# A planned attention + MLP kernel: the operations of pairs 0 to 17 in another order, four norms finished on VectorE, half of the value transfers shortened

## The chip, the cores and the metric

The kernel runs on one core of a Trainium2 chip. The metric is the device time of one execution in microseconds (us). Engines are named as the profile names them: PE (TensorE), ACT (ScalarE), DVE (VectorE), POOL (GpSimd), SP (SyncE, which issues most of the transfers).

## The reference

The first part is cosine attention over 8 batches, 12 heads, 448 positions and 64 dimensions; its output, 3584 rows of 768, goes through an MLP of width 2048 with a hard-swish between.

```python
q_n = q / (np.linalg.norm(q, axis=-1, keepdims=True) + 1e-06)
k_n = k / (np.linalg.norm(k, axis=-1, keepdims=True) + 1e-06)
scores = np.matmul(q_n, k_n.transpose(0, 1, 3, 2)) / tau        # tau = 0.1
attn = np.exp(scores - scores.max(-1)); attn /= attn.sum(-1) + 1e-09
x = (attn @ v).transpose(0, 2, 1, 3).reshape(3584, 768)
h = x @ w_in                                                    # 768 -> 2048
out = (h * np.clip(h + 3.0, 0.0, 6.0) / 6.0) @ w_out            # 2048 -> 768
```

## The kernel before, in words

Two heads form a pair, so there are 48 pairs, six to a batch. Two consecutive pairs share two items of load: an item is a 128 x 2 x 7 x 64 fp32 tile with q (or k) of four heads, 448 KB. Up to item 13 the even item holds q and the odd one k; from item 14 on it is the other way round.

An item goes through these steps, each with a name that the plan uses:

- LQ loads the item (SP). There are seven buffers.
- SQ squares it, on ACT, POOL or DVE (letter a, p or v). Items 0 and 1 are squared in parts.
- RE sums the squares over 64 dimensions (DVE).
- NO makes 1/(norm + eps) for both items of a pair of items, from the sums: on ACT as Ln, Exp(0.5 x), Ln(x + eps), Exp(-x), four small instructions. With the letter v, the last two are an addition and a reciprocal on DVE.
- NM multiplies the item by it and casts it to bf16 (POOL or DVE).
- TR transposes it on PE into a PSUM bank (items 0 to 13), and CQ, CK and CS copy q and k of a pair from there into SBUF. From item 14 on, XD transposes by a DMA on SP.

A pair then has four scores matmul groups SC (groups 0 to 2 with two matmuls of 64 rows, group 3 with the last 64 keys of both heads), four exponentials EX (ACT), four value groups VA (PE, summed in the one PSUM tile PV), FI (DVE: reciprocal of the sums and the product), and BK/CX, XB or XP, which bring the result transposed into xT, the MLP's input. The values of two pairs are loaded by LV in four transfers (SP; three buffers) and cast per pair by VC (POOL, ACT or DVE).

The MLP comes in units U: the first kind is six matmuls of 448 columns for 128 of the 2048 features of a batch, then UA (ACT: relu) and UV (DVE: product); the second kind multiplies by w_out. W issues one of eight weight transfers, 768 KB each as bf16, on POOL's queue. The first four bring w_in: eight units of a batch need the first two, the others need all four. WS and GL prepare sums of w_out and of the hidden activations, with which pairs of output tiles are later computed by seven products instead of eight (L740).

DP.n and D.n are n dummy matmuls on zeros (L922, 248 columns, and L917, 512 columns). Nothing reads their results.

The order of everything up to pair 17 is written out by hand in PLAN, one token for each operation (SQ.5.a.0.7: item 5 on ACT, chunks 0 to 6). Every engine, and SP's queue of transfers, takes its operations in the plan's order, and starts one when the data, buffers and banks that it needs are there. `needs` asserts that the plan's order is a possible one. OPEN ends the first part, in which scores use two double banks SC; behind it scores, transposes and units take six PSUM banks in turn (`next_bank`). From pair 18 on (FIRST) a loop emits a fixed pattern with the units of a table. The plan contains 36 units: 16 of batch 0, 14 of batch 1, six of the second kind.

Of the kernel before, what the change touches and what calls it, by code (L numbers as in the profile page):

```python
# [18 lines left out]
ORDER = "111111111111111111111111111111222222"  # L19

PLAN = [
# [36 lines left out]
]  # L58


# [1 line left out]
def kernel(  # L62
# [76 lines left out]
    def raw_buffer(j):  # L139
# [1 line left out]

    sqs = [item(NR + i) for i in range(2)]
    nrms = [const.tile([128, 7, 2, D], BF16, name=f"nrm{i}", tag=f"nrm{i}") for i in range(3)]
    n2s = [const.tile([128, 2, 14], FP32, name=f"n2{i}", tag=f"n2{i}") for i in range(2)]
    rs = [
        [const.tile([128, 2, 14], FP32, name=f"{x}{i}", tag=f"{x}{i}") for x in ("ln", "nr", "le", "r")]
        for i in range(2)
    ]
    bias = const.tile([128, 2], FP32, name="bias", tag="bias")
    eps_bias, half_bias = bias[:, 0:1], bias[:, 1:2]  # L150
# [50 lines left out]
    def load_v(d):  # L201
        needs(("VC", 2 * (d - NV)), ("VC", 2 * (d - NV) + 1))
        b, n = 2 * d // HP, 2 * d % HP
        for g in range(2):
            f = v[b, HP * g + n : HP * g + n + 2].rearrange("i (p c) d -> p i (c d)", c=7)
            t = vr[d % NV][:, 2 * g : 2 * g + 2, :, :].rearrange("p i c d -> p i (c d)")
            for half in range(2):
                o = t[64 * half : 64 * half + 64, :, (1 - half) * D : (5 - half) * D]
                nc.sync.dma_start(out=o, in_=f[:, :, 3 * half * D : (3 * half + 4) * D])

    def square(j, e, c0, n):

# [15 lines left out]
    def reduce(j, *heads):  # L228
        d = j // 2
        needs(("NO", d - 2, 1))  # L230
        sq, have = sq_of[j]
        heads = heads or (0, 1)
        if j < 2:
            assert all(7 * g + c in have for g in heads for c in range(7))
        else:
            assert sorted(have) == list(range(7))
        c = slice(7 * heads[0], 7 * heads[-1] + 7)
        nc.vector.tensor_reduce(  # L238
            out=n2s[d % 2][:, j % 2, c],
            in_=sq[:, :, :, :].rearrange("p g c d -> p (g c) d")[:, c, :],  # L240
            axis=AX.X,
            op=ALU.add,
        )
        whole("RE", j, heads)

    def norms(d, *items):
        on_vector, items = "v" in items, tuple(x for x in items if x != "v")

        needs(("NM", 2 * d - 4), ("NM", 2 * d - 3))
        items = items or (0, 1)  # L250
        for x in items:
            needs(("RE", 2 * d + x))
        it = slice(items[0], items[-1] + 1)
        ln, nr, le, r = (t[:, it, :] for t in rs[d % 2])
        nc.scalar.activation(out=ln, in_=n2s[d % 2][:, it, :], func=AF.Ln)
        nc.scalar.activation(out=nr, in_=ln, func=AF.Exp, scale=0.5)
        if on_vector:
            nc.vector.tensor_scalar(out=le, in0=nr, scalar1=EPS, scalar2=None, op0=ALU.add)
            nc.vector.reciprocal(out=r, in_=le)
        else:  # L260
            nc.scalar.activation(out=le, in_=nr, func=AF.Ln, bias=eps_bias)
            nc.scalar.activation(out=r, in_=le, func=AF.Exp, scale=-1.0)  # L262
        for x in items:
            issued.add(("NO", d, x))

    def normalise(j, e, *heads):
        d = j // 2
# [6 lines left out]
        engines[e].tensor_tensor(  # L274
            out=nrm[:, :, g, :].rearrange("p c g d -> p g c d"),
            in0=raw_of[j][:, g, :, :],
            in1=rs[d % 2][3][:, j % 2, :]
            .rearrange("p (g c) -> p g c", g=2)[:, g, :]
            .to_broadcast([128, n, 7, D]),
            op=ALU.mult,  # L280
# [31 lines left out]
        return 4 if j % 2 else 2  # L312

    def transposes(j, bank=None):
        nrm = nrm_of.pop(j)
        z, key = bank_of(bank, readers(j))
        z = z[:, :].bitcast(BF16)
# [622 lines left out]
    def whole_units(n, engines="av"):  # L940
# [4 lines left out]
                    finish_units(e)  # L945

    OPS = {
        "LQ": load_qk, "LV": load_v, "W": next_weights, "SQ": square, "RE": reduce, "NO": norms,
        "NM": normalise, "VC": vcast, "TR": transposes, "XD": crossbar, "XB": back_crossbar, "XP": back_two, "CQ": copy_q, "CK": copy_k, "CS": copy_k3, "SC": scores,
        "EX": exps, "VA": values, "FI": finish_values, "BK": back, "CX": copy_x, "U": unit, "UA": lambda: finish_units("a"), "UV": lambda: finish_units("v"),  # L950
        "GL": g_left, "WS": lambda x, *h: weight_sums(str(x), *((h[0] * KC // 2, KC // 2) if h else (0, KC))), "UU": whole_units, "D": busy, "DP": busy_pv, "OPEN": open_ring,
# [146 lines left out]
```

## Time and profile before

| | |
|---|---|
| median of 3 runs | 405.82 us (405.77 to 408.14) |
| profiled execution: span from the first to the last instruction | 403.1 us (the page gives no total beside it) |
| PE busy, of the span | 395.5 us, 98% |
| DVE, ACT, POOL busy | 286.4, 278.3, 234.0 us |
| TensorE clock granted | 1.00 |
| DMA | 65.32 MB, 91566 packets |
| value transfers | 96 of 128 KB, 4.4 us to landing (median) |
| w_in transfers | 4 of 768 KB, 10.2 us to landing (median) |

Busy times are those of one execution. A line such as `L226 POOL TENSOR_TENSOR` names the line of the kernel, the engine and the instruction; in a timeline the first column is the start in us from the beginning of the span, the second is the time from there to the end of the last one of `xN` merged instructions, and what stands in brackets is the engine's idle time before it and what ended it.

### The profile page before, as it was taken

Reading aid. Unit: us, or ns where it says so; the run is one execution under the profiler, and the core shown is the slowest. Engines: PE = TensorE matmul, PEld = TensorE weight load, DVE = VectorE, ACT = ScalarE, POOL = GpSimd, SP = SyncE. Lnnn points to the kernel's source line nnn. Section 1 sums busy time; section 2 is a strip of 40 time slices with the busy share of each in tenths; the row PEclk is TensorE's granted clock in tenths of the full one; section 3 lists DMA queues with packets and bytes.
Section 4 is the critical chain, followed back from the end, with each engine's and each line's share of the span. In section 5 each row is a group of like instructions: output and inputs, shape, how many; then the busy total and the mean of one; then the engine's idle time right before and its main releaser. Section 6 shows DMA issues by size and latency. Waiting matters only on the chain.

```text
span 403.1 us, 9619 instructions
## 1 busy us (share of the span) xinstructions
PE 395.5 (98%) x3696; PEld 234.3 (58%) x3696; DVE 286.4 (71%) x503; ACT 278.3 (69%) x609; POOL 234.0 (58%) x228
## 2 busy tenths in 40 slices
PE   7999999999999999999999999999999999999996
PEld 4666656555655556556555556555565556555563
DVE  5898768766998777776867888687656566644663
ACT  5999998798467686786858768668658755225230
POOL 7799655662384997488386865766665500510070
PEclk9999999999999999999999999999999999999999
DMA  8999989979988659786989659976963523130134
GB/s 289 281 254 257 216 247 230 156 125 230 187 213 220 139 128 228 171 222 130 180 216 212 152 130 164 182 192 145 192 154 76 112 46 67 41 79 21 26 73 99
DMA packets 91566, 65.32 MB, mean 162 GB/s; under 512 B 56064, under 2 KB 89984, under 8 KB 91520
## 3 DMA queue, kind: packets, MB, share of 16 engines
q1 hardware_dynamic: 87408, 58.02, 62.8%
q0 software_dynamic: 3712, 6.29, 9.0%
q8 instruction: 29, 0.48, 0.5%
q10 hardware_dynamic: 400, 0.39, 0.3%
q14 instruction: 17, 0.14, 0.1%
HBM read 47.19 MB, written 11.01 MB: 144 GB/s over the span
## 4 chain that ended last, share of the span: by engine, by line
PE 94%; DVE 3%; DMA 1%; ACT 0%; issue 0%; DVEq 0%; ACTq 0%
PE M L567 24%; PE M L740 17%; PE PV L462 13%; PE Y L567 6%; PE M L422 6%; PE Z L567 5%; PE Y L740 4%; PE Z L740 4%; PE M L614 3%; PE M L820 2%; PE Z L422 2%; PE PV L922 2%; PE Z L820 1%; PE Y L422 1%; DVE n L238 1%; PE SC L422 1%
## 5 line engine op out<-in xcount | busy, mean ns | idle before, releaser
L440 ACT ACTIVATE at<-M 128x448 bf16<-128x448 f32 x200 | 99.9, 568 | 16.4 <-PE M L422 14.4
L567 PE MATMUL M<-xT,w_in_sb 128*128 128x448 bf16 x522 | 110.8, 352 | 0.0
L567 PEld LDWEIGHTS <-w_in_sb 128*128 128x128 bf16 x768 | 72.0, 98 | 62.6 <-issue 2.8
L274 POOL TENSOR_TENSOR nrm<-big,r 128x896 bf16<-128x896 f32 (+1 forms) x48 | 79.5, 1662 | 26.1 <-ACT r L262 19.3
L576 ACT ACTIVATE u<-M,bias 128x448 bf16<-128x448 f32 x87 | 57.0, 655 | 25.2 <-PE M L567 24.8
L582 DVE SCALAR_TENSOR_TENSOR gT<-u,M 128x448 bf16<-128x448 bf16 x76 | 46.7, 618 | 36.8 <-ACT u L576 36.3
L226 POOL TENSOR_TENSOR big<-big 128x896 f32<-128x896 f32 (+3 forms) x39 | 63.9, 1641 | 10.9 <-DMA big<-in_k_dram 5.7
L462 PEld LDWEIGHTS <-at 128*128 128x128 bf16 (+1 forms) x1536 | 54.9, 97 | 22.8 <-issue 13.5
L462 PE MATMUL PV<-vx,at 128*128 128x65 bf16 (+1 forms) x1536 | 64.3, 194 | 0.2 <-DVE on L483 0.2
L238 DVE TENSOR_REDUCE n<-big 128x14 f32<-128x896 f32 (+1 forms) x50 | 51.7, 1041 | 5.6 <-ACT big L224 4.6
L379 POOL COPY km<-tT 64x128 bf16<-64x128 bf16 x34 | 12.8, 376 | 58.1 <-DMA tT<-nrm 45.1
L769 POOL TENSOR_TENSOR big<-big 128x384 f32<-128x384 f32 x11 | 11.8, 1076 | 54.6 <-ACT big L788 54.5
L740 PEld LDWEIGHTS <-gT 128*128 128x128 bf16 x288 | 27.8, 98 | 20.0 <-DVE gT L718 0.6
L740 PE MATMUL M<-w_out_sb,gT 128*128 128x384 bf16 x208 | 37.9, 326 | 0.1
L440 ACT ACTIVATE at<-Z 128x448 bf16<-128x448 f32 x49 | 27.7, 565 | 9.9 <-PE M L422 7.3
L483 DVE TENSOR_TENSOR on<-PV,rc 128x512 bf16<-128x512 f32 x48 | 33.2, 691 | 1.7
L293 POOL CAST vx<-big 128x512 bf16<-128x512 f32 x44 | 33.2, 757 | 1.2 <-DMA big<-in_v_dram 1.1
L422 PE MATMUL M<-tT,kz 64*128 64x448 bf16 (+1 forms) x175 | 31.6, 351 | 0.0
L740 PEld LDWEIGHTS <-gs 128*128 128x128 bf16 x224 | 21.5, 98 | 14.8 <-DVE gs L718 0.4
L567 PE MATMUL Y<-xT,w_in_sb 128*128 128x448 bf16 x132 | 28.6, 352 | 0.0
L440 ACT ACTIVATE at<-Y 128x448 bf16<-128x448 f32 x45 | 25.7, 570 | 3.1 <-PE Z L422 1.7
L740 PE MATMUL M<-w_sum,gs 128*128 128x384 bf16 x144 | 26.3, 326 | 0.0
(130 smaller groups left out, 561.7 us busy)
## 6 DMA issues: line engine op xcount, KB each, us to landing
big<-in_v_dram SPq DMA_DIRECT2D x96, 128.0 KB, 4.4
big<-in_k_dram SPq DMA_DIRECT2D x24, 448.0 KB, 4.9
big<-in_q_dram SPq DMA_DIRECT2D x24, 448.0 KB, 4.4
out_dram<-o SPq DMA_DIRECT2D x107, 96.0 KB, 2.2
w_in_sb<-in_moe_w_in_dram POOLq DMA_DIRECT2D x4, 768.0 KB, 10.2
w_out_sb<-in_moe_w_out_dram POOLq DMA_DIRECT2D x4, 768.0 KB, 9.2
tT<-nrm SPq DMA_TRANSPOSE x34, 3.3
xT<-on SPq DMA_TRANSPOSE x25, 3.8
```

Source lines behind the costliest of these rows:

```text
L226: engines[e].tensor_tensor(out=o, in0=i, in1=i, op=ALU.mult)
L238: nc.vector.tensor_reduce(out=n2s[d % 2][:, j % 2, c], in_=sq[:, :, :, :].rearrange("p g c d -> p (g c) d")[:, c, :], axis=AX.X, op=ALU.add,)
L274: engines[e].tensor_tensor(out=nrm[:, :, g, :].rearrange("p c g d -> p g c d"), in0=raw_of[j][:, g, :, :], in1=rs[d % 2][3][:, j % 2, :] . ...
L293: (engines[e].copy if e == "a" else engines[e].tensor_copy)(out=o, in_=f)
L422: nc.tensor.matmul(o, ks, qt[rows], start=True, stop=True)
L440: nc.scalar.activation(out=o, in_=x, func=AF.Exp, scale=inv_tau)
L462: nc.tensor.matmul(pv_out(j, h), at[rows, n, q_cols(i // HP, j)], vt[rows, 3 + h if name == "M" else 5 * h + int(name[1]), :], start=(name ...
L483: nc.vector.tensor_tensor(out=on[:, :, :, :].rearrange("p j h d -> p h j d"), in0=pv4[:, :, :, 0:D], in1=rc[:, :, :].to_broadcast([128, 2, ...
L567: nc.tensor.matmul(ps[:, 0:S], w_in_sb[:, cc, fc * 128 : (fc + 1) * 128], x[:, cc, 0:S], start=(cc == 0), stop=(cc == CC - 1),)
L576: nc.scalar.activation(out=u[:, :], in_=ps[:, 0:S], func=AF.Relu, bias=half_bias, scale=1.0 / 6.0)
L582: nc.vector.scalar_tensor_tensor(out=g[:, fc, c0 : c0 + S], in0=u[:, :], scalar=1.0, in1=ps[:, 0:S], op0=ALU.min, op1=ALU.mult,)
L740: nc.tensor.matmul(m, lhs[:, c, :], rhs[:, c, c0 : c0 + width], start=(base is None and c == 0), stop=(c == KC - 1), skip_group_check=True,)
```

## The change

1. The tokens of PLAN stand in another order. The first lines, up to OPEN, were

```diff
-    "LQ.1 DP.5 SQ.1.a.11.3 SQ.1.p.4.3 DP.1 SQ.1.a.0.4 LQ.0 SQ.0.p.8.6 DP.2 DP.4 LQ.3 LQ.2 SQ.1.v.7.4 RE.1.1",
-    "SQ.0.a.0.6 RE.1.0 NO.0.1 LQ.5 LQ.4 SQ.0.v.6.2 DP.6 NM.1.p.0 D.10 RE.0.1 DP.3 NM.1.p.1 RE.0.0 DP.8 NO.0.0",
-    "SQ.3.a.0.7 LV.0 DP.2 SQ.2.a.0.7 NM.0.p.0 RE.3 RE.2 NM.0.p.1 TR.1.Y DP.2 TR.0.Z CK.0.v DP.4 SQ.4.p.0.7 CQ.0.v",
-    "SQ.5.a.0.7 LQ.6 NO.1 LV.1 LQ.7 SC.0.0.0 SC.0.1.1 DP.5 DP.3 CQ.1.v EX.0.0 RE.5 RE.4 NM.3.p SC.0.2.0 CK.1.v DP.3",
-    "EX.0.1 DP.3 EX.0.2 NM.2.v DP.3 SC.0.3.1 TR.3.Y LQ.8 NO.2 EX.0.3 DP.3 SC.1.0.0 TR.2.Z EX.1.0 VC.0.v SC.1.1.1 DP.2",
-    "EX.1.1 VA.0.0 CK.2.v VC.1.v VC.3.v NM.4.p NM.5.p VA.0.1 LQ.9 SC.1.2.0 SQ.6.a.0.7 LQ.11 DP.5 DP.2 SC.1.3.1 EX.1.2",
-    "CQ.2.v LQ.10 LV.2 VA.0.2 VA.0.3 DP.3 SC.2.0.0 DP.2 EX.1.3 CK.3.v SC.2.1.1 EX.2.0 TR.4.Y SC.2.2.0 SQ.7.p.0.7",
-    "EX.2.1 RE.6 FI.0 RE.7 LV.3 VA.1.0 SQ.8.p.0.7 SC.2.3.1 CQ.3.v VC.2.v CQ.5.v VA.1.1 EX.2.2 SC.3.0.0 EX.2.3 VA.1.2",
-    "NO.3 RE.8 SC.3.1.1 CQ.4.v EX.3.0 DP.2 DP.4 EX.3.1 VA.1.3 TR.5.Z SC.3.2.0 W SQ.9.p.0.7 EX.3.2 FI.1 CK.4.v BK.0.Y",
-    "VA.2.0 SC.3.3.1 RE.9 LV.4 EX.3.3 NO.4 VA.2.1 VA.2.2 VA.2.3 SC.4.0.0 EX.4.0 NM.6.p DP.2 SC.4.1.1 SQ.10.p.0.7 W",
-    "SQ.11.p.0.7 EX.4.1 CX.0.v TR.6.Y CK.5.v FI.2 CQ.7.v VA.3.0 BK.2.Z RE.10 SC.4.2.0 EX.4.2 NM.7.p CQ.6.v VA.3.1",
-    "SC.4.3.1 DP.2 EX.4.3 CX.2.v SC.5.0.0 RE.11 VA.3.2 EX.5.0 SC.5.1.1 VA.3.3 VC.4.p SC.5.2.0 FI.3 VC.5.p EX.5.1",
-    "BK.1.Y TR.7.Z SC.5.3.1 CX.1.v CK.6.v CK.7.v VA.4.0 EX.5.2 DP.2 CS.7.v EX.5.3 BK.3.Y VA.4.1 LQ.12 CS.6.v OPEN",
+    "LQ.1 SQ.1.a.11.3 LQ.0 LQ.3 LQ.2 SQ.1.p.4.3 SQ.1.a.0.4 DP.8 LQ.5 SQ.1.v.7.4 SQ.0.a.0.6 RE.1.1 DP.2 DP.4 RE.1.0",
+    "DP.6 LQ.4 DP.5 SQ.0.p.8.6 SQ.0.v.6.2 DP.2 NO.0.1 SQ.3.a.0.7 D.10 RE.0.1 DP.3 RE.0.0 NM.1.p.0 DP.1 NO.0.0.v",
+    "NM.1.p.1 NM.0.p.1 DP.4 DP.5 SQ.2.a.0.7 DP.2 TR.1.Y RE.3 DP.3 NM.0.p.0 DP.3 LV.0 RE.2 LV.1 SQ.5.a.0.7 CK.0.v",
+    "TR.0.Z SQ.4.p.0.7 LQ.6 CQ.0.v RE.5 DP.1 CQ.1.v DP.2 SC.0.0.0 NO.1 DP.4 RE.4 EX.0.0 SC.0.1.1 SC.0.2.0 CK.1.v",
+    "NM.2.v EX.0.1 NM.3.p SC.0.3.1 LQ.7 VC.3.a DP.3 NO.2.v EX.0.2 DP.5 NM.4.p VC.1.v VC.0.v LQ.10 EX.0.3 TR.3.Y DP.1",
+    "SC.1.0.0 EX.1.0 SC.1.1.1 TR.2.Z VA.0.0 LQ.8 SC.1.2.0 SQ.6.v.0.7 EX.1.1 CK.2.a VA.0.1 SC.1.3.1 NM.5.p EX.1.2 LQ.9",
+    "VA.0.2 DP.3 CQ.2.v LQ.11 LV.2 EX.1.3 CQ.3.v SC.2.0.0 EX.2.0 VA.0.3 CK.3.v SC.2.1.1 TR.4.Y SQ.7.p.0.7 SC.2.2.0",
+    "RE.6 FI.0 RE.7 DP.1 VA.1.0 DP.3 SQ.8.p.0.7 EX.2.1 CQ.4.v CQ.5.v SC.2.3.1 TR.5.Z RE.8 EX.2.2 NO.3 VA.1.1 DP.1",
+    "EX.2.3 SC.3.0.0 EX.3.0 VA.1.2 DP.1 W VC.2.v VA.1.3 FI.1 SC.3.1.1 SC.3.2.0 BK.0.Y EX.3.1 SQ.9.p.0.7 SQ.10.p.0.7",
+    "DP.1 CK.4.v EX.3.2 SC.3.3.1 VA.2.0 RE.9 LV.3 EX.3.3 DP.4 VA.2.1 VA.2.2 SC.4.0.0 VA.2.3 NO.4 CK.5.v NM.6.p RE.10",
+    "DP.1 EX.4.0 SC.4.1.1 EX.4.1 SC.4.2.0 CX.0.v FI.2 TR.6.Y VA.3.0 SQ.11.p.0.7 BK.2.Z NM.7.p EX.4.2 SC.4.3.1",
+    "SC.5.0.0 VA.3.1 VA.3.2 W EX.4.3 EX.5.0 CX.2.v VC.4.p SC.5.1.1 RE.11 CQ.7.v LQ.12 EX.5.1 VA.3.3 SC.5.2.0 EX.5.2",
+    "TR.7.Z CQ.6.v FI.3 SC.5.3.1 BK.1.Y DP.3 VC.5.p CS.7.v EX.5.3 CX.1.v CS.6.v CK.6.v VA.4.0 VA.4.1 BK.3.Y OPEN NO.5",
     ...
```

The rest of the plan is reordered in the same way. The first unit stands behind SC.8.2 in both.

2. Some operations have another engine. To DVE's side: the norms NO.0.0, NO.2, NO.9 and NO.10 end there; SQ.6 (from ACT), NM.13, NM.14 and VC.13 (from POOL), CQ.11 and CK.12 (from ACT). To ACT: VC.3, CK.2, CK.15, CK.16 and CQ.10 (from DVE), VC.12, VC.15 and SQ.21 (from POOL). To POOL: a seventh of SQ.16 (from ACT). There are 82 narrow dummy matmuls instead of 86.

3. The value transfers leave out the 64-dimension blocks that no cast reads:

```diff
             for half in range(2):
-                o = t[64 * half : 64 * half + 64, :, (1 - half) * D : (5 - half) * D]
-                nc.sync.dma_start(out=o, in_=f[:, :, 3 * half * D : (3 * half + 4) * D])
+                n_c = 4 if g == half else 3
+                c0 = (7 - n_c) * half
+                x = 1 if g != half or half == 0 else 0
+                o = t[64 * half : 64 * half + 64, :, x * D : (x + n_c) * D]
+                nc.sync.dma_start(out=o, in_=f[:, :, c0 * D : (c0 + n_c) * D])
```

4. The five small tiles of a norm hold both of the alternating sets in one tile each, and the four instructions stand in a function of their own. `norms_two` is there but the plan has no token for it.

```diff
-    n2s = [const.tile([128, 2, 14], FP32, name=f"n2{i}", tag=f"n2{i}") for i in range(2)]
-    rs = [
-        [const.tile([128, 2, 14], FP32, name=f"{x}{i}", tag=f"{x}{i}") for x in ("ln", "nr", "le", "r")]
-        for i in range(2)
+    n2_and_r = [
+        const.tile([128, 2, 2, 16], FP32, name=x, tag=x)[:, :, :, 0:14] for x in ("n2", "ln", "nr", "le", "r")
     ]
...
+        inverse([t[:, d % 2, it, :] for t in n2_and_r], on_vector)
...
+    def inverse(tiles, on_vector):
+        n2, ln, nr, le, r = tiles
+        nc.scalar.activation(out=ln, in_=n2, func=AF.Ln)
         nc.scalar.activation(out=nr, in_=ln, func=AF.Exp, scale=0.5)
         if on_vector:
             nc.vector.tensor_scalar(out=le, in0=nr, scalar1=EPS, scalar2=None, op0=ALU.add)
             nc.vector.reciprocal(out=r, in_=le)
         else:
             nc.scalar.activation(out=le, in_=nr, func=AF.Ln, bias=eps_bias)
             nc.scalar.activation(out=r, in_=le, func=AF.Exp, scale=-1.0)
```

More of the change, by code (lines that the diff above doesn't have):

```diff
@@ L238, in reduce @@
         nc.vector.tensor_reduce(
-            out=n2s[d % 2][:, j % 2, c],
+            out=n2_and_r[0][:, d % 2, j % 2, c],
             in_=sq[:, :, :, :].rearrange("p g c d -> p (g c) d")[:, c, :],
@@ L253, in norms, with norms_two @@
         it = slice(items[0], items[-1] + 1)
-        ln, nr, le, r = (t[:, it, :] for t in rs[d % 2])
-        nc.scalar.activation(out=ln, in_=n2s[d % 2][:, it, :], func=AF.Ln)
+        inverse([t[:, d % 2, it, :] for t in n2_and_r], on_vector)
+        for x in items:
+            issued.add(("NO", d, x))
+    def norms_two(d, on_vector=None):
+        needs(*(("NM", 2 * d + x) for x in range(-4, 0)), *(("RE", 2 * d + x) for x in range(4)))
+        inverse([t.rearrange("p e i c -> p (e i) c") for t in n2_and_r], on_vector)
+        issued.update(("NO", x, y) for x in (d, d + 1) for y in range(2))
+    def inverse(tiles, on_vector):
+        n2, ln, nr, le, r = tiles
+        nc.scalar.activation(out=ln, in_=n2, func=AF.Ln)
         nc.scalar.activation(out=nr, in_=ln, func=AF.Exp, scale=0.5)
@@ L262, in norms @@
             nc.scalar.activation(out=r, in_=le, func=AF.Exp, scale=-1.0)
-        for x in items:
-            issued.add(("NO", d, x))
     def normalise(j, e, *heads):
@@ L276, in normalise @@
             in0=raw_of[j][:, g, :, :],
-            in1=rs[d % 2][3][:, j % 2, :]
+            in1=n2_and_r[4][:, d % 2, j % 2, :]
             .rearrange("p (g c) -> p g c", g=2)[:, g, :]
@@ L314, in transposes @@
     def transposes(j, bank=None):
+        needs(("NM", j))
         nrm = nrm_of.pop(j)
@@ L947 @@
     OPS = {
-        "LQ": load_qk, "LV": load_v, "W": next_weights, "SQ": square, "RE": reduce, "NO": norms,
+        "LQ": load_qk, "LV": load_v, "W": next_weights, "SQ": square, "RE": reduce, "NO": norms, "NN": norms_two,
         "NM": normalise, "VC": vcast, "TR": transposes, "XD": crossbar, "XB": back_crossbar, "XP": back_two, "CQ": copy_q, "CK": copy_k, "CS": copy_k3, "SC": scores,
```

46 rows, old and new, of the table PLAN are left out of this document.

## The prediction

> **What bounds the kernel now.** I read the page's head first, then the busy time in three stages, the timelines of PE and POOL in the first 45 us, and the time that the weight transfers took to land.
>
> ```profile
> span 403.1 us, 9619 instructions
> PE 395.5 (98%) x3696; PEld 234.3 (58%) x3696; DVE 286.4 (71%) x503; ACT 278.3 (69%) x609; POOL 234.0 (58%) x228
> ```
>
> TensorE is the bound, but "98% busy" hides the one place where something can be won. The stages below run from the first exponential (12.87) to the first MLP unit (42.85), from there to the first score of pair 18 (115.49), and from there almost to the end.
>
> ```profile
> 12.87:42.85 29.98, 29.54 (x420) 19.46 (x418) 25.73 (x60) 28.76 (x58) 28.64 (x23) 1.00 1.08 262
> 42.85:115.49 72.64, 72.64 (x714) 42.43 (x713) 55.09 (x95) 58.41 (x130) 37.85 (x35) 1.00 0.98 198
> 115.49:390.00 274.51, 274.35 (x2442) 160.09 (x2440) 193.74 (x311) 182.23 (x402) 156.10 (x147) 1.00 0.63 139
> ```
>
> The columns are length, then busy us of PE, PEld, DVE, ACT, POOL, the clock, the DMA share, GB/s. From 42.85 on PE has no hole worth a name: units of six matmuls follow at 1.14 us, which is streaming speed, so that stage cannot get shorter. In the first stage ACT (28.76 of 29.98), POOL (28.64) and DMA (share 1.08) are full, and part of PE's 29.54 is filler: 49 dummy matmuls of 0.106 us, 5.2 us in all. So the change can gain only ahead of 42.85, and only if ACT, POOL and the transfers get through their head sooner.
>
> ```profile
> 2.48 3.90 PE L922 MATMUL PV<-xT 128*128 128x248 bf16 x18 [2.48 <-DVE vx L975]
> 6.17 2.78 PE L917 MATMUL Y<-xT 128*128 128x512 bf16 x10
> 8.79 1.54 PE L922 MATMUL PV<-xT 128*128 128x248 bf16 x13
> 10.17 0.55 PE L319 MATMUL Y<-ident,nrm 128*128 128x128 bf16 x7
> ...
> 12.47 0.55 PE L422 MATMUL SC<-tT,kz 64*128 64x448 bf16 x4 [0.65 <-DVE tT L341]
> ...
> 42.85 2.43 PE L567 MATMUL M<-xT,w_in_sb 128*128 128x448 bf16 x12
> ```
>
> Fillers run back to back from 2.48: 0.207 us each at first, 0.106 us (13 from 8.79 to 10.17) once the clock has opened, at about 7.0. The first MLP unit at 42.85 is where the full stretch begins.
>
> ```profile
> 23.07 0.85 POOL L910 DMA_DIRECT2D w_in_sb<-in_moe_w_in_dram  x1
> ...
> 28.86 0.70 POOL L910 DMA_DIRECT2D w_in_sb<-in_moe_w_in_dram  x1
> 29.57 1.69 POOL L226 TENSOR_TENSOR big<-big 128x896 f32<-128x896 f32 x1
> 31.21 1.69 POOL L274 TENSOR_TENSOR nrm<-big,r 128x896 bf16<-128x896 f32 x1
> 32.84 1.16 POOL L293 CAST vx<-big 128x512 bf16<-128x512 f32 x2
> ```
>
> POOL is a closed row of 1.64 us pieces, and the two weight transfers that the first unit needs are issued in it. For the second of them:
>
> ```profile
> L910 POOL DMA_DIRECT2D w_in_sb<-in_moe_w_in_dram x1: 699/699/699, 28.9 to 28.9; - x1
> ...
> DMA to landing us min/median/max: 13.7/13.7/13.7
> ```
>
> 28.86 + 13.7 = 42.56: it landed 0.3 us ahead of the first unit. That cover is all there is.
>
> **The change, part by part.** I walk the new order through the engines with the durations of the rows.
>
> *Fillers ahead of the first score.* Before the first transposes there are now 27 + 10 wide + 15 fillers (18 + 10 + 13 before), then 6 and 3 (2 and 4). PE takes them in order: 22 cold ones to 7.0, five warm to 7.56, ten wide at 0.216 to 9.72, fifteen to 11.31, transposes of item 1 (7 x 0.056) to 11.70, six fillers to 12.34, transposes of item 0 to 12.73. The copy of q starts 0.22 us after the last and takes 0.38, so the first score starts at about 13.43 instead of 12.47: **+0.96**. In the meantime ACT gets its squares and norms done earlier (square of item 3 moves into the 0.74 us that ACT waited for DVE), so it is free at 12.15 and waits for the late score. Of the +0.96 about 0.7 is won back in pairs 0 and 1, because the four-step norm of items 4 and 5 is now two steps on ACT (saves 0.26 + 0.27) and the square of item 6 (0.84) leaves ACT, while a value cast and a key copy come to it (about 0.5 each; ACT's copies take 0.48 to 0.53).
>
> *Norms finished on DVE.* Two small operations of about 0.21 us (reciprocal row, 128x8). For items 4 and 5 they stand behind the 1.2 us normalisation of item 2 in DVE's queue: r is ready at 17.6 instead of 16.4, and POOL, which waits for it, starts item 4 at 17.65 instead of 16.52: **+1.1 on POOL**, whose row is closed after that.
>
> *Square of item 6 on DVE.* Alone it takes 1.08 us (the same operation at 108.68). It has two inputs in SBUF, and such an operation waits for a running POOL operation:
>
> ```profile
> 213.38 0.68 DVE L718 TENSOR_TENSOR gs<-gT 128x1024 bf16<-128x1024 bf16 x1
> ...
> 221.21 1.99 DVE L718 TENSOR_TENSOR gs<-gT 128x1024 bf16<-128x1024 bf16 x1
> ```
>
> 0.68 with POOL idle, 1.99 with POOL working (a square at 220.96, then a normalisation that took 2.14 instead of 1.69). Here POOL is full, so bounds are 0 and 1.3 us for DVE, and 0 and 1.1 us for POOL (one DVE operation). I take 0.5 and 1.1. POOL's square of item 7 then begins at 22.05 instead of 19.81.
>
> *Weight transfers.* The first is issued behind the square of item 8, at 25.3 (23.07 before). The second stood behind the square of item 10; now it also stands behind the square of item 11 and the normalisation of item 7, 2 x 1.64 us: issue at 34.4 instead of 28.86. By the three of four that did not start behind another, landing takes 9.8 to 10.4 us; the second of before landed 9.7 after the first. So it lands at 44.2 to 44.8, I take 44.5, and the first unit starts at 44.6: **+1.75**. The bounds are 7.3 us (the last weight transfer, on an emptier DMA: 41.7, no wait) and 13.7 (48.1, +5.3). The Trainium skill, "DMA: Bandwidth & Descriptors", section on the anatomy of one DMA on the gpsimd path, fits 2.0 us plus bytes at 436 GB/s; for 1.57 MB read that is, as an estimate, 5.6 us and no wait. The rows of this case, 7.3 to 14.4 us, do not agree, and they decide; by the Trainium skill's figure the wait would drop out.
>
> *The other chain to the first unit* (scores of pair 8, whose exponential frees the bank): POOL's lateness reaches the reduction of item 7, so the norms of items 6 and 7 start about 1.1 later and the first exponential of pair 3 is at 26.3 (24.96). ACT is paced from there, so the exponentials of pair 6 start at 37.2 (36.12), and the first unit could start at 43.9. It is hidden behind the weights by 0.7; if they come early, +1.05 is left.
>
> *Value transfers.* 48 of 96 move 96 instead of 128 KB: 1.57 MB of 65.32. Their number, and so SP's issues, stays at 96. Six pairs of heads load ahead of 42.85: 0.39 MB, 1.5 us of a full DMA at 262 GB/s. Only about 0.1 MB falls into the second weight transfer's window, against two q/k loads that now come earlier there. Bounds -0.4 to +0.4 on its landing; I take 0.
>
> *The full stretch.* The instruction order holds the same real matmuls from the first unit to pair 18. Changes between 64-row scores and 128-row work cost 0.1 us each (the last transpose at 17.02 streams 0.06 us, the score behind it starts at 17.17); by the order there are 47 instead of 45 of them: **+0.2**. Two normalisations move from POOL to DVE (1.08 to 2.7 each; DVE has 17 us free there), four casts and copies and a square to ACT (some 2 us net, 14 free). Summed along the order, ACT from the second exponential of pair 8 to the first of pair 11 has 16.8 us against PE's 16.1, but 1.75 us of waiting for the weights lets it catch up. Bounds 0 and 4.3; I take **0.3**.
>
> *Sum:* 1.75 + 0.2 + 0.3 = +2.25 on the span of 403.1, 405.35. The page has no total for this execution; the median 405.82 lies 2.72 above its span. So 405.82 + 2.25 = **408.1**.
>
> **The rivals.**
> 1. *The weights come in time.* As the last two did (7.3 and 7.6 us), they land at 42.0 or sooner; the score chain sets the first unit at 43.9. +1.05 + 0.5: 407.4. For it: fewer value bytes. Against: DMA share 1.08 at that time. The Trainium skill's fit, named above, would give this case too.
> 2. *Faster: ACT's gaps close.* In the first stage ACT was idle 1.22 us of 29.98, and its list gets 0.37 shorter. If it never waits after its start at 13.85 (+0.96), the first unit comes 1.22 + 0.37 - 0.96 = 0.6 us sooner, at 42.2, and with the +0.2 the time is 405.4. It decides if the second weight transfer is issued by 34.4 and lands in under 7.7 us and POOL loses nothing to DVE's square. Against: r for item 4 waits behind a DVE normalisation.
> 3. *The full stretch loses its cover.* ACT's local excess over PE (0.7 up to pair 11, 0.6 in pair 12, 0.8 in pair 15: 2.1 us) and two 1.1 us waits of DVE's moved normalisations land on the bank releases that PE needs: +4.3 - 0.3 on top of the sum, 412.1. For it: ACT at 58.4 of 72.6, uneven. Against: before ran the part up to pair 11 with ACT's sum at 0.96 of PE's, and PE had no such wait.
>
> **How the numbers follow.** Forecast 0.40 (own range 406.6 to 409.9), rival 1 0.20, rival 2 0.11, rival 3 0.29. A measurement of this kernel tells about 1%, 4.1 us, from no change, so forecast and rival 1 count as the same: same 0.65, slower 0.33 (rival 3 and the forecast's upper end), faster 0.02 (PE's full stretch leaves no room for it). Range 405.2 to 412.0: from rival 2 to rival 3, leaving out the upper half of the latter and weights that land as late as 13.7 us.
>
> **What would show it.** The first 64-row score at 13.4, not 12.5; POOL's normalisation of item 4 near 17.6; DVE's square of item 6 over 1.08 us; the second weight issue near 34, its landing near 44.5 and PE's first unit right behind it with a wait on DMA; pair 18's first score near 117.7; from there the same 287 us to the end. A first unit ahead of 42.85, or waits of over 1 us on ACT or DVE behind it, would prove me wrong.

## The result, and the profile after

The changed kernel takes 410.42 us (median of 7 executions, 408.22 to 411.18) against 405.82 of the kernel before on the same chip (7 executions, 404.95 to 408.14): a ratio of 1.0097, 95% interval 1.0069 to 1.0124. The interval leaves out 1, so the loss is real, though it is just under the 1% that the prediction called the same. The forecast of 408.1 is 2.3 us short; 410.42 lies in the range, but outside the forecast's own part of it. The profiled execution took 408.59 and its span is 406.6, against 403.1 before. In the changed kernel the lines of the functions have numbers 11 higher, so the scores are L433 and the MLP's first product is L578.

The head of the page and the three stages, with columns as before (from the first exponential to the first unit, to the first score of pair 18, to almost the end):

```profile
span 406.6 us, 9623 instructions
PE 394.7 (97%) x3692; PEld 234.7 (58%) x3692; DVE 291.1 (72%) x514; ACT 277.9 (68%) x603; POOL 227.8 (56%) x223
```

```profile
13.12:43.62 30.50, 27.76 (x402) 18.26 (x401) 26.54 (x62) 28.50 (x56) 28.30 (x22) 1.00 1.00 260
43.62:119.15 75.53, 73.11 (x715) 42.71 (x714) 58.62 (x104) 58.61 (x127) 32.13 (x33) 1.00 0.93 183
119.15:393.66 274.51, 274.33 (x2443) 160.17 (x2441) 193.17 (x310) 182.48 (x403) 155.17 (x144) 1.00 0.60 135
```

The third window was cut to the length that it had before. What can be compared is the time from pair 18's first score to the end of the span: 287.5 us, against 287.6 before. The first unit comes 0.77 us later (43.62, 42.85 before). The second stage, which "cannot get shorter", got 2.89 us longer (75.53, 72.64 before), and PE is idle in it for 2.4 us where it had no idle time. These 2.4 us, in two pieces, are called the hole below. 0.77 + 2.89 = 3.66 is the delay of pair 18.

The timelines of PE and POOL ahead of the first unit (start, time to the end of the last, in brackets the idle time before):

```profile
2.47 4.60 PE L933 MATMUL PV<-xT 128*128 128x248 bf16 x27 [2.47 <-DVE vx L986]
6.91 2.32 PE L928 MATMUL Y<-xT 128*128 128x512 bf16 x10
9.06 1.75 PE L933 MATMUL PV<-xT 128*128 128x248 bf16 x15
...
12.71 0.36 PE L433 MATMUL SC<-tT,kz 64*128 64x448 bf16 x2 [0.16 <-DVE tT L352]
...
43.62 1.31 PE L578 MATMUL M<-xT,w_in_sb 128*128 128x448 bf16 x6
```

```profile
16.77 4.18 POOL L284 TENSOR_TENSOR nrm<-big,r 128x896 bf16<-128x896 f32 x2 [2.18 <-DVE r L271]
20.92 3.31 POOL L227 TENSOR_TENSOR big<-big 128x896 f32<-128x896 f32 x2
24.18 0.85 POOL L921 DMA_DIRECT2D w_in_sb<-in_moe_w_in_dram  x1
...
33.26 0.70 POOL L921 DMA_DIRECT2D w_in_sb<-in_moe_w_in_dram  x1
```

The two normalisations at 16.77 take 4.18 instead of 3.34: DVE's square of item 6 holds them up. The second weight transfer is issued at 33.26 and lands after

```profile
DMA to landing us min/median/max: 8.4/8.4/8.4
```

at 41.66, two microseconds ahead of the first unit. In the second stage PE's waits, DVE's longest wait (us in total, times, longest), the last two weight transfers, and SP's queue around the two transposes of items 14 and 15 read

```profile
PE Y L433 <- DMA tT<-nrm: 1.4, 1, 1.4
PE PV L473 <- DVE on L494: 0.9, 1, 0.9
```

```profile
DVE kz L380 <- DMA tT<-nrm: 3.5, 1, 3.5
```

```profile
72.72 0.81 POOL L921 DMA_DIRECT2D w_out_sb<-in_moe_w_out_dram  x1
...
75.18 0.81 POOL L921 DMA_DIRECT2D w_out_sb<-in_moe_w_out_dram  x1
```

```profile
76.23 1.34 SPq L341 DMA_TRANSPOSE tT<-nrm  x1
77.67 0.52 SPq L195 DMA_DIRECT2D big<-in_q_dram  x1
78.33 4.20 SPq L341 DMA_TRANSPOSE tT<-nrm  x1
```

and before

```profile
70.41 2.63 SPq L330 DMA_TRANSPOSE tT<-nrm  x2
```

The first transpose landed 8.6 us after its issue, at 84.8, the second 10.1 us after, at 88.4; before, they were issued at 70.41 and 71.8 and landed 6.3 and 5.7 us later. DVE's copy of k of pair 14 waited for the first, so FI of pair 12 behind it was late for the values of pair 13 (0.9); then the scores of pair 14 waited for the second (1.4). Two things now stand ahead of the second transpose: the weights, and the load of item 21 (448 KB, issued at 77.67, landed at 87.5), which the kernel before issues behind both transposes.

### The profile page after: what moved, and what is told of

Same layout as the page of the kernel before. It is cut to its first block, busy times and chain, and to the rows that moved or that the text cites. A ratio compares the mean times of both kernels' runs of the same rounds, so it can differ in the third digit from the quotient of the medians.

```text
span 406.6 us, 9623 instructions
## 1 busy us (share of the span) xinstructions
PE 394.7 (97%) x3692; PEld 234.7 (58%) x3692; DVE 291.1 (72%) x514; ACT 277.9 (68%) x603; POOL 227.8 (56%) x223
## 4 chain that ended last, share of the span: by engine, by line
PE 86%; DMA 4%; DVE 3%; ACT 3%; POOL 2%; issue 1%; SPq 0%; POOLq 0%; ACTq 0%
PE M L578 23%; PE M L751 16%; PE PV L473 11%; PE Y L578 6%; PE M L433 5%; PE Z L578 5%; PE Y L751 4%; PE Z L751 3%; PE M L625 3%; DMA tT<-nrm 2%; PE M L831 2%; PE Z L433 2%; POOL nrm L284 1%; PE Z L831 1%; PE Y L433 1%; DMA big<-in_q_dram 1%
## 5 line engine op out<-in xcount | busy, mean ns | idle before, releaser
L578 PE MATMUL M<-xT,w_in_sb 128*128 128x448 bf16 x516 | 109.4, 352 | 0.2 <-DMA xT<-on 0.2
L451 ACT ACTIVATE at<-M 128x448 bf16<-128x448 f32 x196 | 97.4, 565 | 16.7 <-PE M L433 14.6
L578 PEld LDWEIGHTS <-w_in_sb 128*128 128x128 bf16 x768 | 72.0, 98 | 62.5 <-issue 2.5
L284 POOL TENSOR_TENSOR nrm<-big,r 128x896 bf16<-128x896 f32 (+1 forms) x46 | 76.3, 1662 | 24.3 <-DVE r L271 12.7
L227 POOL TENSOR_TENSOR big<-big 128x896 f32<-128x896 f32 (+4 forms) x39 | 62.9, 1615 | 10.8 <-DMA big<-in_k_dram 7.6
L451 ACT ACTIVATE at<-Z 128x448 bf16<-128x448 f32 x52 | 29.5, 568 | 9.3 <-PE M L433 9.0
L303 POOL CAST vx<-big 128x512 bf16<-128x512 f32 x41 | 29.4, 723 | 8.6 <-DMA big<-in_v_dram 7.5
L433 PE MATMUL M<-tT,kz 64*128 64x448 bf16 x172 | 31.1, 351 | 0.6 <-DVE kz L352 0.5
L578 PE MATMUL Y<-xT,w_in_sb 128*128 128x448 bf16 x132 | 28.6, 352 | 0.0
```

The source lines that it names most:

```text
L227: engines[e].tensor_tensor(out=o, in0=i, in1=i, op=ALU.mult)
L284: engines[e].tensor_tensor(out=nrm[:, :, g, :].rearrange("p c g d -> p g c d"), in0=raw_of[j][:, g, :, :], in1=n2_and_r[4][:, d % 2, j % 2, :]
L303: (engines[e].copy if e == "a" else engines[e].tensor_copy)(out=o, in_=f)
L433: nc.tensor.matmul(o, ks, qt[rows], start=True, stop=True)
L451: nc.scalar.activation(out=o, in_=x, func=AF.Exp, scale=inv_tau)
L578: nc.tensor.matmul(ps[:, 0:S], w_in_sb[:, cc, fc * 128 : (fc + 1) * 128], x[:, cc, 0:S], start=(cc == 0), stop=(cc == CC - 1),)
```

## The experiments

Two questions: what makes the hole at 85 to 88 us, and what sets the first unit. All ratios are to the kernel before in the same set of runs. A loss in the full stretch is pair 18's first score minus the first unit, less the 72.64 us of before.

**e1: the last two weight transfers late.** The changed kernel, with the last two W moved back.

```diff
-SQ.16.p.0.6 UA EX.13.0 W UV U RE.16 U
+SQ.16.p.0.6 UA EX.13.0 UV U RE.16 U
-EX.13.2 UA W VC.14.p UA NO.8 SC.13.3 CS.14.v NM.16.p EX.13.3
+EX.13.2 UA VC.14.p UA NO.8 SC.13.3 CS.14.v W NM.16.p W EX.13.3
```

> The changed kernel, with the last two w_out transfers issued behind the transposes of items 14 and 15 (before the k copy of pair 14 and behind the normalisation of item 16) instead of ahead of them. Theory A (the hole of 2.7 us on PE at 85.5 to 88.5 comes from the transfers that fill the DMA engines while the two transposes wait): the second transpose lands within 7 us instead of 10.1, the hole is gone, and the time falls by 2.5 us from 410.4 to about 407.9, 1.005 of before. Theory B (the transposes are late because DVE finishes item 14 only at 76.2, 2.04 us with a wait for POOL, and the weights have nothing to do with it): the hole stays, 410.4.

408.24, ratio 1.0066 (1.0049 to 1.0084). The transposes, issued at 76.0 and 78.0 as late as before the edit, now landed in 2.6 to 4.5 us and the hole is gone. But 2.28 us of the full stretch stay lost: PE waits for DVE, 0.9 us up to 97.6 and 0.5 up to 101.7. So the transfers' place explains the hole, and moving them alone gives most of it back later. In the profile's chain of what released what, the first of these waits goes back to

```profile
88.98 7.35 DMA tT<-nrm
```

This is the next transpose. It landed at 96.33, just behind the last weight transfer, which was issued at 87.17 and landed at 95.36; in the changed kernel, with no weights ahead of it, it took 2.7 us. DVE's copy out of it stands ahead of the product that PE waits for. So the same collision came back one pair of items later.

**e2: item 14 normalised on POOL.** The changed kernel with `NM.14.p` for `NM.14.v`.

> The changed kernel, with one letter changed: item 14 is normalised on POOL again. The transpose of item 14 is then issued near 71.5 instead of 76.2, and POOL issues the last two w_out transfers 1.6 us later. Theory A (DMA engines full of weights): the first transpose lands before the weights flow, the second partly; the hole shrinks to 0 to 1 us, 408 to 409. Theory B (late normalisation): the hole is gone, 407.8. If moving it costs POOL something elsewhere, 410 or more.

406.78, ratio 1.0034 (1.0021 to 1.0047). The transposes were issued at 71.8 and 73.8 and landed by 80.8; the loss of the full stretch is 0.30, less than either theory gave. The last two weight transfers now went out behind the transposes, at 74.8 and 77.2. One letter gives back 0.63% of the 0.97%.

**e3: the kernel before with the last two W early**, right behind its NM.15.p.

> The kernel before, with the last two w_out transfers issued directly behind the normalisation of item 15 (near 67) instead of at 78.0 and 85.7; nothing else. Theory A: the transposes of items 14 and 15, issued at 70.4 and 71.7, no longer land in 5.7 to 6.8 us but only when the weights are through, near 85 to 88; PE gets a hole of 1 to 4 us ahead of the scores of pair 14, and the time is 407 to 410. Theory B: no change, 405.8.

405.71, ratio 1.0009 (0.9986 to 1.0031). The transposes landed 11.8 and 12.4 us after their issue at 71.9 and 73.3, at 84.3 and 85.1, slower than in any other run: as in theory A, they landed only when the weights were through (84.2). The full stretch lost 1.10 in the profile, with 0.9 us of waiting on PE, but the median does not show it.

**e4: the kernel before with the shortened value transfers alone** (part 3 of the change).

> The kernel before with the shortened value transfers alone (48 of 96 move 96 instead of 128 KB). The forecast took this part at nothing: 405.8, within 0.4 us. Rival: the DMA engines, full up to the first MLP unit, get through sooner, weights land up to 1.5 us earlier and the head shortens: 404.8 to 405.3.

405.36, ratio 0.9999 (0.9982 to 1.0016): nothing, within 0.7 us.

**e7 and e8: the hole rebuilt in the kernel before.** e7 has the late normalisation alone, e8 also the early transfers.

```diff
-UA NM.14.p SQ.16.p.0.6 U UA
+UA SQ.16.p.0.6 U UA
-SC.13.0 SQ.17.p.0.7 XD.14 UV RE.17 EX.12.3 VC.12.p EX.13.0
+SC.13.0 SQ.17.p.0.7 UV NM.14.v RE.17 EX.12.3 VC.12.p EX.13.0
-UV XD.15 UA U UA
+UV XD.14 XD.15 UA U UA
 (e8 only)
-SQ.17.p.0.7 UV NM.14.v RE.17 EX.12.3 VC.12.p EX.13.0
+SQ.17.p.0.7 W UV NM.14.v RE.17 EX.12.3 VC.12.p W EX.13.0
-EX.13.2 UV NO.8 W U SC.13.3
+EX.13.2 UV NO.8 U SC.13.3
-EX.14.1 UV U W SC.14.3
+EX.14.1 UV U SC.14.3
```

> The kernel before with one thing of the change: item 14 normalised on DVE, behind the reductions near 74 instead of on POOL at 68.7, so that both transposes by DMA of items 14 and 15 are issued near 77 instead of 70.4 and 71.7; the weight transfers stay at 78.0 and 85.7. Theory (late transposes and weights ahead of them in the DMA are needed together): the transposes land in 3 to 7 us, by 82 to 84, and PE waits 0 to 1 us; 405.4 to 406.5. Rival (lateness alone does it): a hole of 2 us or more behind 84 and 407.5 to 408.5.

> The kernel before with item 14 normalised late on DVE as in the kernel labelled e7, and with the last two weight transfers issued ahead of both transposes (near 73 and 75, instead of 78.0 and 85.7), as the changed kernel has them. Theory (both together make the hole): the transposes land 8 to 12 us after their issue, the copy of k of pair 14 waits 3 us or more for the first, holes of 2 to 3.5 us in PE between 83 and 90, 407.8 to 409. If the hole in the changed kernel had another cause (its other order of units, or casts on DVE), the time stays under 406.7 and the holes under 1 us.

e7: 406.23, ratio 1.0009 (0.9989 to 1.0030), transposes issued at 75.8 and 77.2, landed in 2.6 us each, loss 0.34. e8: 406.79, ratio 1.0038 (1.0007 to 1.0070), issued at the same time, landed in 8.8 and 8.1 us, loss 1.28. The landings are as expected, the loss is not: PE waits 1.0 us in all, and both this and the time are at the edge of what would have spoken for another cause (1 us, 406.7). The early weights do most of it: alone, in e3, they cost 1.10, and the late normalisation alone, in e7, 0.34. And the second transpose landed at 85.3, 0.8 us behind the first; in the changed kernel it landed at 88.4, 3.6 us behind the first and 0.9 behind the load of item 21. In e8 that load is issued behind both transposes. In e1, without weights ahead, the load between them still made the second take 4.5 us where the first took 2.6. So the rest of the changed kernel's hole is put down to the load's place by these landings; no run moved the load alone.

What the weights do to SP's queue can be seen in the DMA queues of the changed kernel between 78 and 84 us (packets, MB, share of the time of 16 engines; then the issue and us to landing):

```profile
q0 software_dynamic: 694, 1.02, 93.5%
q1 hardware_dynamic: 863, 0.23, 24.1%
...
tT<-nrm SPq DMA_TRANSPOSE x1, 10.1
```

q0 carries the weights, q1 all that SP issues. While the weights flow, q1 gets about as many packets as q0 (863 to 694) but a quarter of the time: by these figures its packets hold some 270 bytes, those of the weights 1470. In the same 6 us of e7, with weights for a part of it, q1 moved 0.69 MB instead of 0.23. The Trainium skill, "DMA: Bandwidth & Descriptors", section on queues, rings and completion order, states that an engine takes the queues in turn, a whole packet at a time; these counts agree with it.

**e9: is it DVE's blocked queue?** The changed kernel, with the copies of k of pair 14 behind FI of pair 12.

```diff
-U CK.14.v VA.12.2 UA UV VA.12.3
+U VA.12.2 UA UV VA.12.3
-SC.13.3 CS.14.v NM.16.p EX.13.3 FI.12 LV.8 U
+SC.13.3 NM.16.p EX.13.3 FI.12 CK.14.v CS.14.v LV.8 U
```

> The changed kernel with one thing moved: DVE's copy of k of pair 14 (with POOL's copies of the same pair) stands behind the product that finishes pair 12 instead of ahead of it, so that DVE's queue isn't held for 3.5 us by the late transpose. Theory that the landing of the second transpose (88.4 in the changed kernel) sets the hole: the first hole (1.09 us at 85.4, values waiting for DVE) goes, the second (1.58 us at 86.9, scores of pair 14 waiting for the transpose) grows by as much; 2.2 to 3.2 us in all, pair 18's first score 75.1 to 76.1 behind the first unit, time within 0.8 of the changed kernel's 410.4. Rival, that the loss comes from DVE's blocked queue: the first hole goes and the second doesn't grow; pair 18 at 74.0 to 74.6 behind the first unit, 408.9 to 409.5.

411.18, ratio 1.0122 (1.0095 to 1.0149). The wait on DVE is gone and the wait for the second transpose, which landed at 88.8, is one hole of 2.6 us: its landing sets the hole, the blocked queue only divides it. The full stretch lost 4.34, though, more than either theory gave. PE's timeline and the windows around the hole (busy times of PE, PEld, DVE, ACT, POOL, then the granted clock) show the rest:

```profile
88.91 0.53 PE L433 MATMUL Y<-tT,kz 64*128 64x448 bf16 x1 [2.59 <-DMA tT<-nrm]
...
89.41 2.42 PE L578 MATMUL M<-xT,w_in_sb 128*128 128x448 bf16 x6
```

```profile
88.20:88.40 0.20, 0.00 (x0) 0.00 (x0) 0.20 (x1) 0.00 (x0) 0.07 (x1) 1.00 1.53 316
88.40:88.60 0.20, 0.00 (x0) 0.00 (x0) 0.17 (x1) 0.00 (x0) 0.00 (x0) 0.56 0.78 148
...
91.60:91.80 0.20, 0.20 (x4) 0.18 (x3) 0.00 (x0) 0.00 (x0) 0.16 (x1) 0.50 0.18 63
91.80:92.00 0.20, 0.20 (x11) 0.20 (x9) 0.00 (x0) 0.14 (x1) 0.20 (x1) 0.91 0.17 63
```

From 88.4 to 91.8 the clock was granted at half, and a unit of six matmuls took 2.42 instead of 1.31 us. PE worked for 2.9 of these 3.4 us, so that half the clock cost about 1.5 us, an estimate. The profiled execution of the changed kernel, with its hole in two pieces, kept the clock at 1.00 there.

**e5: fewer fillers.** e2 with 15 of the narrow dummy matmuls ahead of the first score left out (`DP.8` to `DP.5`, `DP.6` to `DP.3`, and so on).

> The changed kernel with item 14 normalised on POOL (the kernel that measured 406.78, U1 at about 43.8), and 15 of the narrow dummy matmuls ahead of the first score and among the first scores left out (nothing reads them). Theory of the prediction, that PE's fillers hold back the first score: the transposes of item 0 then wait only for its normalisation (ended 11.5), the first score comes at about 12.2 instead of 12.67, and the first unit at 43.3 to 43.5; 406.3 to 406.5. Rival, that POOL and ACT set the head and the fillers cost nothing: first score earlier by up to 0.5, first unit within 0.15 of 43.8, 406.6 to 406.9. Third, that PE's clock opens later without them (fewer matmuls, more idle): transposes and scores slower, first score not earlier, 407 or more.

406.84, ratio 1.0028 (1.0001 to 1.0054). First score at 12.24 (12.67 in e2, 12.71 in the changed kernel), first unit at 43.23 (44.02, 43.62). In the profile the fillers cost 0.4 on the first score; the median does not tell e5 from e2.

**e6: two engine moves of the head undone.** e2 with `NO.2` for `NO.2.v` and `SQ.6.a` for `SQ.6.v`.

> The changed kernel with item 14 normalised on POOL, and two engine moves of the head undone: the norms of items 4 and 5 end on ACT again (two small instructions instead of DVE's two), and the square of item 6 is on ACT (0.84 us) instead of DVE. Theory of the prediction, that POOL's closed row (item 4 waiting for r behind DVE's normalisation, and POOL held up 0.85 by DVE's square) sets the first unit: POOL's square of item 7 about 1.1 earlier (20.1 instead of 21.2), first unit at 42.9 to 43.1, 405.9 to 406.1. Rival, that ACT's row of exponentials sets it and the moves only shift work: ACT gets 0.84 + 0.5 more ahead of the exponentials of pair 1, first unit at 44.2 to 45.0, 407.2 to 408. If both are equally tight: 43.8 within 0.3, 406.8.

408.23, ratio 1.0041 (1.0023 to 1.0058), first unit at 44.64. POOL was not held up any more, its square of item 7 came at 20.75 (21.20 in e2), and yet the unit came later, as in the rival on ACT's row. Part of that may be PE's clock, which opened later in this execution (first score at 13.16), so the unit is better counted from POOL, below.

**e10: the second w_in transfer sooner.** e5 with W moved from behind VA.3.2 to behind SQ.9.p.

> The kernel labelled e5 (item 14 on POOL, fewer fillers: first unit at 43.23, 406.84) with the second w_in transfer issued one square earlier twice over, near 26.5 instead of 32.9. Theory of the prediction's main term (the transfer's landing can set the first unit): in the profile of e5 it landed at 40.6 and cannot gain, but in executions in which landing takes 10.4 us or more it did set it, so the first unit stays at 43.0 to 43.4 and the median falls by up to 0.5, to 406.3 to 406.8. Rival (weights never matter, and two transfers at once slow the loads of q and k): the first unit at 43.4 to 44.2 and 406.9 to 407.6.

407.39, ratio 1.0024 (1.0006 to 1.0042), first unit at 45.12. Most of the delay is older than the moved transfer: already the first transfer went out at 25.17 instead of 23.80, because a square on POOL had waited 1.3 us for its load at 12.96. The other 0.5 us comes behind the moved issue, which takes 0.70 us of POOL's row. It gained nothing.

**e11 and e12: ACT relieved in the kernel before**, `SQ.6.v` and `NO.2.v`; e12 also issues the second W behind SQ.9.p.

> The kernel before with two of the changed kernel's engine moves alone: the square of item 6 on DVE instead of ACT, and the norms of items 4 and 5 finished on DVE. ACT has 0.84 + 0.5 us less ahead of the first unit, DVE 1.7 + 0.5 more, POOL is held up about 0.85 by DVE's square. Theory that ACT's row of exponentials sets the score chain: scores of pair 8 up to 1 us sooner, but the second weight transfer, issued up to 1 us later than 28.86 and landing in 9 to 13.7 us, now sets the first unit: 42.3 to 43.5, time 405.0 to 406.5. Theory that POOL's row sets the chain: first unit 43.5 to 44.0, 406.5 to 407.

> The kernel labelled e11 with the second w_in transfer issued behind the square of item 9, near 26 to 27, instead of behind that of item 10. If ACT sets the score chain and the weights are out of the way: first unit at 41.7 to 42.4, 404.6 to 405.4, the fastest of all. If POOL's row sets it: 43.0 or later, 406 or more. If the two weight transfers together starve the loads of q and k: first unit past 43.5.

e11: 406.78, ratio 1.0020 (0.9998 to 1.0041), first unit at 45.73, in an execution whose third square on POOL waited for its load until 13.67 (11.90 before). e12: 406.84, ratio 1.0021 (0.9998 to 1.0044), first unit at 43.94. In e12, DVE's square and POOL's two squares behind it:

```profile
18.53 2.42 DVE L226 TENSOR_TENSOR big<-big 128x896 f32<-128x896 f32 x1
```

```profile
19.97 4.34 POOL L226 TENSOR_TENSOR big<-big 128x896 f32<-128x896 f32 x2
24.25 0.85 POOL L910 DMA_DIRECT2D w_in_sb<-in_moe_w_in_dram  x1
```

4.34 instead of 3.32: 1.02 lost on POOL, and the first unit came 1.09 later than before, ACT's relief notwithstanding. Which row carries the delay these two runs do not tell. POOL is late, but the profile's chain runs through DVE: in e12 through this square, the reductions and FI behind it, to a score that starts at 24.73 instead of 23.64, 1.09 later. That is ahead of the moved transfer, issued at 26.75, so it is not the two transfers together that cost the time. None of the twelve versions beat the kernel before.

**What sets the first unit.** POOL issues the first weight transfer right behind its early row. Over all the profiles, the first unit stands at a nearly fixed distance behind that issue (us):

| kernel | first W issued | first unit | distance |
|---|---|---|---|
| before, e3, e7, e8 | 22.99 to 23.09 | 42.77 to 42.87 | 19.78 |
| e11, e12 | 26.05, 24.25 | 45.73, 43.94 | 19.68, 19.69 |
| e4 | 24.41 | 44.34 | 19.93 |
| changed, e1, e5, e9 | 24.18, 24.01, 23.80, 24.57 | 43.62, 43.45, 43.23, 43.99 | 19.42 to 19.44 |
| e2 | 24.46 | 44.02 | 19.56 |
| e10 (a second W, 0.70, early in the row) | 25.17 | 45.12 | 19.95 |
| e6 (square of item 6 on ACT) | 24.37 | 44.64 | 20.27 |

So the two move together, over a spread of three microseconds. That alone does not say that POOL's row sets the unit: in the kernel before, e3, e7 and e8 the first score keeps as fixed a distance to it (30.38), and in e11 and e12 DVE is late with POOL. The profile's chain has to decide. In the changed kernel, e1, e2, e5 and e9 it runs through POOL's row and from there to the reduction of item 7 and ACT's norms and exponentials; in the changed kernel with

```profile
16.77 4.04 POOL nrm L284 x2
20.92 1.69 POOL big L227
```

There POOL's early row sets the first unit. In the kernel before the chain between 8 us and the unit has no piece of POOL, and in e4, e10 and e11 it begins with a load of q that came late. Two rows of the table stand apart. In e2 the second transfer took 10.4 us and landed at 43.9, 0.1 us ahead of the unit. In e6 the distance is 0.83 longer and the chain runs from the late first score through ACT's row, with the square that ACT got back; how much of the 0.83 is the square and how much the late clock was not separated.

## Why the prediction was right and wrong

**Fillers, +0.96.** Right in kind, a quarter in size. The first score came at 12.71, 0.24 later than before, not at 13.43 (to which the terms add up only with 0.1 us more; they give 13.33). The clock opened at 5.7 and not at the 7.0 that I copied from the trace of before, so more fillers ran at 0.106 us. The moment differs between executions: 5.4 to 6.6 us in e1, e2, e6 and e9, which have the same fillers, and in e6 the first 27 took 5.04 us instead of 4.60. A sum over cold and warm matmuls must carry that as a bound.

**POOL's item 4, +1.1, and the lock of DVE's square, +1.1.** The first was 0.25 (16.77 against 16.52), because DVE had r ready at 16.7 and not at 17.6; the second was 0.85. Together 1.1, and the first weight transfer is 24.18 - 23.07 = 1.11 late. e12 confirms the price of the lock (1.02 on POOL, 1.09 on the first unit); that POOL's row is the one that counts here is what the changed kernel's chain shows. The new order behind it wins back 0.34 (19.44 instead of 19.78), and 1.11 - 0.34 is the measured 0.77. I had put this chain at 43.9 and called it hidden; it was the bound, at 43.62.

**Weight transfers, +1.75: the step that failed first.** The issue was at 33.26 (34.4 forecast) and landing took 8.4 us, not 10. Over the profiles of the changed head it took 7.7 to 10.4 us, and even at 10.4 (e2) it landed ahead of the unit. PE waited for it in none. I chose the upper rows of before; the rival with the weights in time had the right reading of the head, 0.77 for its 1.05.

**The full stretch, +0.2 and +0.3: the step that failed worst.** It lost 2.89. In e2, e5, e6 and e10, which have the new order without the hole, it lost 0.30 to 0.32 with PE idle for 0.08: that is the 0.2 forecast for the transitions, and less than the 0.3 beside it. The hole is the rest. I costed item 14's normalisation on DVE as engine time (it did take 2.04 instead of 1.08), and never walked what it issues: the two transposes behind it on SP's queue. The change moved them from 70.4 and 71.8 to 76.2 and 78.3, and moved the last two weight transfers ahead of them, from 78.0 and 85.7 to 72.7 and 75.2. I followed the first two W transfers through the queues and not the last two.

For the landing of the transposes it counts which weight transfers are ahead of them, and not how late they are issued. In thirteen of the fourteen profiles weights were under way when the first transpose was issued. In eleven of these it landed 0.2 to 1.0 us behind the last weight transfer issued ahead of it: before at 76.7 behind 76.0, in the changed kernel at 84.8 behind 84.2, in e3 at 84.3 behind 84.2, though issued 4 us sooner. Where that transfer was nearly through, it took 2.6 us (e5, and e7 with its late transposes). In the changed kernel the late normalisation cost as much as it did because it put the transposes behind the last two weight transfers; e2 takes it away and the hole is gone. The load of item 21 between the transposes, which I did not walk either, kept the second until 88.4.

**The third rival** (loss of cover) had the right stage and, at 412.1, a price 1.7 us above the median, but other causes: ACT's excess over PE, of which none of PE's waits in the full stretch shows anything, and DVE's moved normalisations.

**Luck.** The forecast has the head 0.98 us too long and the full stretch 2.39 too short. That it misses the median by only 2.3 us owes something to these two errors against each other, since the clock, below, adds to the second. That the time lies in the range is due to the upper end, which was drawn for the third rival and its other causes.

**The median against the profiled execution.** I added the change of the span to a median 2.72 above the profiled span. But an execution's time lies only 1.9 to 2.1 above its own span in the changed kernel (408.59 - 406.6), and 1.7 to 1.9 in the kernel before: its profiled execution was a short one, and some 0.2 us of the loss lie outside the spans. What makes the median 1.8 higher than the profiled execution is most likely the clock: five of the seven executions, 410.26 to 411.18, have a mean granted clock of 0.994 to 0.996, the two others, 408.22 and 408.59, have 0.998. e9's profile shows the place at which it is lost (0.994 to 0.996 in all six of its executions); e8 has 0.994 to 0.996 in the four of its twelve that took 409.49 to 411.04, and e2, without a hole, in none of six. A few executions of other kernels have such a clock too (two of twelve in e5, at 0.995), and that the five lost it at the hole was not traced.

**Value transfers, 0, and the tail, 287 us.** Both right, the first within e4's interval: e4 measured 0.9999, and from pair 18 on the length is 287.5 (406.6 - 119.15) against 287.6.

## What to carry to other kernels

When an operation moves to a later time or another engine, follow what it issues through every queue, and look at what else is moved ahead of it there, on its own queue and on others: here weights on one queue held back small transposes on another until the weights were through, and a load between two transposes held back the second. Cost a stall at a full TensorE by its length and by what it may do to the clock behind it. Where many chains meet, look over several profiles for events that keep a fixed distance to the one that matters, and then ask the chain of releases which of them carries it: two rows that hold each other up are late together.

## What the runs showed of the hardware

- Transposes by DMA, 2.6 us to landing without weight transfers beside them, took 8.1 to 12.4 us behind two of 768 KB on the software queue, whose packets took 93.5% of the engines' time from 78 to 84 us. The first of the two landed 0.2 to 0.7 us behind the second weight transfer.
- With a 448 KB load on SP's queue between two transposes the second landed 3.6 us behind the first, with the load behind both 0.8 (changed kernel and e8, both behind weights).
- In e9 PE's clock was halved for 3.4 us; the hole, 2.6 us in all, had lasted 2.1 us at the switch. In the 3.4 us up to the switch at 88.4, PE had been busy for about 1.3 us. The Trainium skill, "TensorE: Matmul & The Clock Gate", Part 1, asks for one idle window of about 3.4 us, free-running; the length of the slow stretch agrees, the idle window here was not wholly idle.
- DVE's square with two operands in SBUF beside POOL's took 2.42 us and lengthened POOL's by 1.02 in e12; in the changed kernel it took 1.67 and lengthened POOL's by 0.85. So how the wait is divided between the two differs from case to case.
- The second w_in transfer, the same in size and place, took 8.4, 8.7, 10.4 and 7.7 us to land in the profiles of the changed kernel, e1, e2 and e5.
- PE's clock opened between 5.1 (e11) and 8.3 us (e8) after the span's start in the fourteen profiles, with the first matmul at 2.5 in all of them.
